# A gated delta-rule layer with a gated MLP on one core: U of the first group in two buffers of its own, weight loads sent behind its copy, fewer dummy products

## The chip, the cores and the metric

The kernel runs on one NeuronCore of a Trainium2 chip. The metric is device time in microseconds of one execution, the median of several runs. TensorE is written PE here (its weight loads PEld), VectorE DVE, ScalarE ACT, GpSimd POOL; SP issues the DMAs.

## The reference

```python
def _attn_ref(q, k, v, beta):               # (4, 8, 768, 48), beta (4, 8, 768)
    k_n = k / (np.linalg.norm(k, axis=-1, keepdims=True) + 1e-06)
    for t in range(S):
        y[:, :, t] = np.einsum('bhd,bhde->bhe', q[:, :, t], state)
        v_old = np.einsum('bhde,bhd->bhe', state, kt)
        state = state + bt[:, :, :, None] * np.einsum('bhd,bhe->bhde', kt, vt - v_old)

def _moe_ref(x, w_gate, w_val, w_out):      # x (3072, 384), d_ff 1536
    gate = 1.0 / (1.0 + np.exp(-(x @ w_gate)))
    val = x @ w_val
    return (gate * val @ w_out)
```
The output of the delta rule, all heads side by side, is the input of the MLP.

## The kernel before

The 768 tokens of each of 32 heads are cut into 12 groups of 64 (`g`, with g = 0 the first). Within a group the recurrence is solved in closed form: products of keys with keys (`gram`, L317), their norms (`norms`, L252), an inverse of a triangular matrix on DVE (`solve_halves`, L410, for groups 0 to 2), and then the corrected values U in two half steps (`updates`, L500): step 0 multiplies the inverse with the first half rows (PE, L518, tile `pu`) and copies them (L521) to `su`; step 1 takes their part from the second half (L510, tile `pk`; `less`, L495, on DVE); step 2 does the second half as step 0 did the first. `su` also holds the state, in the other 64 rows. `rows` (L523) multiplies masked key-query products with `su` for the outputs (tile `yy`, L539), `flip` (L565) transposes them (tile `pt`, L574), `advance` (L547) makes the next state.

The MLP of a group runs tile by tile over d_ff: `gate_val` (L608; tile `gv`, L615 in group 0 and L618 later), sigmoid and product (`gated`, L620), `outp` (L636). One tile is two slots of the loop at L868: in an even slot `gate_val`, in an odd one `outp` of two tiles before. While the MLP of one group runs, the recurrence of the next groups is placed between, by the tables `plan`, `late` and `tail` (L662 to L858). Each table entry names a slot. All orders are written by hand (`manual_schedule`, L699): each engine does its instructions in the order in which the code emits them.

Group 0 has no MLP ahead of it. What PE does there is emitted at L699 to L759, and dummy products (`busy_array`, L102: a bf16 weight load and a product of 512 columns whose result is not used) stand in its idle times. Eight of them are paced: each waits for one instruction of the solve on DVE (`paced`, L448).

The weights come as 36 pieces of 384 KB (`load_piece`, L185), numbered from 0, in the order gate, value, output of each tile. Pieces 0 to 9 are sent at the start. From then on `scaled(n)` (L201, two ACT instructions that unpack piece n) sends piece n + BEHIND, if that is at least EAGER (L209); pieces 10 to 13 are sent behind the copy of U in step 2 (L747). `in_turn` (L111) keeps the number of transfers under way down: from L746 on each waits for the third last one to land. `scaled(n)` of pieces 10 to 35 stand in slots 0 to 18 (L761).

In the trace an f32 product counts as two pairs of weight load and matmul (so the 32 products of a `pu` step are 64 matmuls); a bf16 or f32r one as one pair.

Of the kernel before, what the change touches and what calls it, by code (L numbers as in the profile page):

```python
# [30 lines left out]
J = 8  # L31
# [29 lines left out]
def deltanet_gated_mlp(ctx: ExitStack, tc: tile.TileContext, kd, qd, kv, beta, words, out):  # L61
# [40 lines left out]
    def busy_array(out, n, after=()):  # L102

        for i in range(n):
            ins = nc.tensor.matmul(out=out.rearrange("q a b -> q (a b)"), lhsT=flat[:, 0:128], rhs=flat, start=True, stop=True)  # L105
            if i < len(after):
                pace(ins, after[i])

    sent, behind = [], []

# [299 lines left out]
    def solve_halves(g):  # L410
# [36 lines left out]
        if g == 0:  # L447
            paced = beats[14::2]  # L448
            busy_array(pz, len(paced) + 3, after=paced)
# [13 lines left out]
        if g == 0:  # L463
            gap.append(ps_gv.tile([128, J, C], F32, name="gap", tag="gv"))
            busy_array(gap[0], 3)
        yield
# [4 lines left out]
    def rest(g):  # L471

        st = state[g]
        kq, V = kqp[g % 2], st["kv"][:, 1]
        st["pk"] = pk = [ps_seq.tile([128, J, D], F32, name=f"pk_{g}_{e}", tag="seq") for e in range(2)]
        if g == 0:
            for e in range(2):
                nc.tensor.matmul(out=pk[e].rearrange("q j d -> q (j d)"), lhsT=flat[:, 0:128], rhs=su[:, 2].rearrange("q j d -> q (j d)").bitcast(BF16)[:, 0:J * D],
                                 start=True, stop=True, skip_group_check=True)
        n = 32 if g == 1 else 64  # L480
        for j in range(J if g else 0):
            for a in range(0, 64, n):
                for e, x in KINDS:
                    r, t = 64 * e, tokens_at(e, x) + a
                    m = D // 2 if g == 1 and a == 0 and 0 < j < 4 else D
                    for d in range(0, D, m):
                        nc.tensor.matmul(out=pk[e][t:t + n, j, d:d + m], lhsT=kq[r:r + D, x, j, a:a + n], rhs=su[r:r + D, 2 * x + e, j, d:d + m],  # L487
                                         start=j == 0, stop=True, skip_group_check=True)
        if g == 0:
            st["R"] = [V[:, e * J:(e + 1) * J] for e in range(2)]  # L490
        else:
            st["R"] = [wk.tile([128, J, D], F32, name=f"R_{g}_{e}", tag="row", bufs=3) for e in range(2)]
            less(g)
# [6 lines left out]
    def updates(g, step):  # L500
# [5 lines left out]
        if step == 1:  # L506
            for j in range(J):
                for e, x in KINDS:
                    one, two = to[e, x][0], at[e, x][1]
                    nc.tensor.matmul(out=st["pk"][e][two:two + 32, j], lhsT=L[one:one + 32, x * J + j], rhs=su[one:one + 32, 2 * x + e, j],  # L510
                                     start=False, stop=True, skip_group_check=True)
            less(g)
            return
        pu = [ps_aux.tile([128, J, D], F32, name=f"pu_{g}_{step}_{x}", tag="aux") for x in range(2)]
        for j in range(J):
            for e, x in KINDS:
                i, r = at[e, x][step // 2], to[e, x][step // 2]
                nc.tensor.matmul(out=pu[x][r:r + 32, j], lhsT=mt[i:i + 32, e * J + j], rhs=R[e][i:i + 32, j], start=True, stop=True)  # L518
        for e, x in KINDS:
            r = to[e, x][step // 2]  # L520
            st["u"] = (nc.vector.tensor_copy if g == 0 and x else nc.scalar.copy)(out=su[r:r + 32, 2 * x + e], in_=pu[x][r:r + 32])  # L521

    def rows(g):  # L523
# [7 lines left out]
        n = 32  # L531
        for e in range(2):
            for x in range(2):
                for pair in zip(order[::2], order[1::2]):
                    for a in range(0, 64, n):
                        for j in pair:
                            b, h = head_of(e, x, j)
                            lo = 64 * (b % 2) + a
                            nc.tensor.matmul(out=py[e][lo:lo + n, b // 2, h // 2], lhsT=kq[:, 2 + 2 * e + x, j, a:a + n], rhs=su[:, 2 * x + e, j], start=True, stop=True)  # L539
        st["ys"] = ys = wk.tile([128, 2, H // 2, 2, D], F32, name=f"ys_{g}", tag="ys", bufs=1)  # L540
# [6 lines left out]
    def advance(g):  # L547
# [4 lines left out]
        if 1:  # L552
            pd = [ps_seq.tile([128, J, D], F32, name=f"pd_{g}_{t}", tag="seq") for t in range(2)]
            for j in range(J):
                for e, x in KINDS:
                    r, t = 64 - tokens_at(e, x), below(e)
                    nc.tensor.matmul(out=pd[e][r:r + D, j], lhsT=Kt[t:t + 64, x * J + j], rhs=su[t:t + 64, 2 * x + e, j], start=True, stop=True)  # L557
            for e, x in KINDS:
# [135 lines left out]
    joins, splits = joining(), splitting()  # L694
    EAGER, BEHIND = 14, 8

# [16 lines left out]
    gap.append(ps_gv.tile([128, J, C], F32, name="early", tag="gv"))  # L713
    busy_array(gap.pop(), 5)
    norms0, norms1 = norms(0), norms(1)
# [19 lines left out]
    updates(0, 0)  # L735
    busy_array(gap[0], 5)
    lower_left(1)
# [10 lines left out]
    load_k(2)  # L748
    busy_array(gap[0], 5)
    scaled(9)  # L750
# [18 lines left out]
    spread(splits, 3, 24, 29, into=tail)  # L769
    spread(splits, len(pieces) + 1 - 15, 29, 44, into=tail)  # L770
    tail[18].append(behind.clear)
    for part in (1, 0):
# [144 lines left out]
```

## Time and profile before

| what | before |
|---|---|
| median of 3 runs | 628.56 us (628.52 to 628.64) |
| the profiled execution | 628.08 us |
| its span, first to last instruction | 626.4 us |
| mean granted TensorE clock | 0.996 |
| weight loads sent (36), median from issue to landing | 4.4 us |

A row of the chain of waits gives a start, a length, and the engine, tile and line that held the end; "issue" in it is time in which PE waited for nothing that the profile shows. A row of a timeline gives start, length, engine, line, operation, output and input with their shapes, the count, and in brackets the idle time before it with what ended it. Matmul ends are modelled.

### The profile page before, as it was taken

The numbers are of one execution on the slowest core, as the hardware profiler recorded it, in microseconds if no ns is written. First come the engines' busy times: TensorE is split into PE (matmuls) and PEld (weight loads), VectorE is DVE, ScalarE is ACT, GpSimd is POOL, SyncE is SP. The second block draws the span as 40 slices with busy tenths as digits, with TensorE's granted clock in tenths as the row PEclk, the third lists the DMA queues.
The fourth block names the chain that finished last, engine by engine and source line by source line (L and its number), as shares of the span: only waits on it lengthen the run. The fifth ranks groups of instructions, "written<-read, shape, count | busy, mean of one in ns | idle before, by whom it ended". The sixth has DMA issues, their size and how long they took to land.

```text
span 626.4 us, 25310 instructions
## 1 busy us (share of the span) xinstructions
PE 609.4 (97%) x11126; PEld 565.4 (90%) x11126; DVE 474.4 (76%) x1423; ACT 340.1 (54%) x907; POOL 43.9 (7%) x105
## 2 busy tenths in 40 slices
PE   5889999999999999999999999999999999999996
PEld 4467778899999999999999999999999999999996
DVE  5878786698869879878978978977977977953221
ACT  6759866466446446446446446456456456435322
POOL 6100000000002002002002002002002002001000
PEclk9899999999999999999999999999999999999999
DMA  9478832102112113113113113113113100100101
GB/s 274 170 228 265 281 93 76 31 4 87 28 31 85 27 29 87 26 29 87 27 29 87 27 29 87 27 29 87 27 28 88 27 3 3 26 4 3 26 1 25
DMA packets 17774, 41.14 MB, mean 66 GB/s; under 512 B 4224, under 2 KB 7296, under 8 KB 17664
## 3 DMA queue, kind: packets, MB, share of 16 engines
q1 hardware_dynamic: 17664, 39.53, 21.9%
q8 instruction: 87, 1.43, 1.0%
q14 instruction: 23, 0.19, 0.1%
HBM read 34.80 MB, written 4.72 MB: 63 GB/s over the span
## 4 chain that ended last, share of the span: by engine, by line
PE 90%; DVE 4%; ACT 3%; POOL 1%; issue 1%; ACTq 0%; POOLq 0%
PE gv L618 44%; PE po L649 21%; PE gv L615 5%; PE pu L518 3%; PE yy L539 3%; PE po L643 3%; PE pg L328 2%; PE pp L356 2%; PE pk L487 2%; PE pk L510 1%; PE pd L557 1%; DVE w L236 1%; PE gap L105 1%; PE pm L446 1%; ACT kv L309 1%
## 5 line engine op out<-in xcount | busy, mean ns | idle before, releaser
L618 PE MATMUL gv<-xx,w 128*128 128x256 f32 x2376 | 311.6, 285 | 0.3 <-DVE xx L580 0.3
L618 PEld LDWEIGHTS gv<-xx,w 128*128 128x128 f32 x2376 | 298.9, 191 | 4.0 <-DVE xx L580 0.6
L649 PE MATMUL po<-w,h 128*128 128x384 f32 x792 | 162.7, 341 | 0.0
L649 PEld LDWEIGHTS po<-w,h 128*128 128x128 f32 x792 | 133.8, 188 | 1.2
L629 ACT CAST h<-sg 128x256 fp32r<-128x256 f32 x132 | 53.5, 405 | 116.5 <-DVE sg L624 116.1
L623 ACT ACTIVATE sg<-gv 128x256 f32<-128x256 f32 x144 | 54.9, 381 | 113.1 <-PE gv L618 103.2
L624 DVE TENSOR_TENSOR sg<-sg,gv 128x256 f32<-128x256 f32 x144 | 60.1, 417 | 65.3 <-ACT sg L623 65.0
L384 DVE TENSOR_TENSOR tmp<-X,gp 128x126 f32<-128x126 f32 (+22 forms) x279 | 73.3, 263 | 8.2
L387 DVE TENSOR_TENSOR X<-X,tmp 128x126 f32<-128x126 f32 (+22 forms) x279 | 72.4, 259 | 8.4
L634 DVE TENSOR_TENSOR h<-sg,h 128x256 fp32r<-128x256 f32 x132 | 54.9, 416 | 12.5 <-ACT h L629 12.4
L594 POOL COPY x<-yt 32x192 f32<-32x192 f32 x72 | 29.8, 413 | 443.9 <-DVE yt L589 441.3
L521 ACT COPY su<-pu 32x384 f32<-32x384 f32 x92 | 43.3, 470 | 10.8 <-PE pu L518 9.0
L309 ACT ACTIVATE kv<-kv,mq 128x48 f32<-128x48 f32 x160 | 40.3, 325 | 0.0
L361 DVE TENSOR_TENSOR kqp<-pp,pmask 64x512 f32<-64x512 f32 x48 | 33.0, 689 | 1.4
L615 PE MATMUL gv<-xx,u 128*128 128x256 f32 x144 | 33.7, 385 | 0.1
L615 PEld LDWEIGHTS gv<-xx,u 128*128 128x128 f32 x144 | 26.6, 190 | 4.7 <-ACT xx L577 0.6
L498 DVE TENSOR_TENSOR R<-kv,pk 128x384 f32<-128x384 f32 x44 | 22.4, 550 | 10.0 <-PE pk L510 9.3
L340 ACT COPY G<-pg 32x256 f32<-32x256 f32 (+1 forms) x69 | 25.3, 367 | 7.8 <-PE pg L328 6.4
L594 ACT COPY x<-yt 32x192 f32<-32x192 f32 x72 | 25.1, 349 | 1.2
L589 DVE STREAM_TRANSPOSE yt<-ys 128x768 f32<-128x768 f32 x9 | 8.8, 979 | 20.0 <-ACT ys L545 20.0
L229 ACT CAST w<-u 128x384 fp32r<-128x384 f32 x36 | 18.0, 508 | 9.3 <-DVE w L236 9.2
L563 DVE TENSOR_TENSOR su<-su,pd 48x384 f32<-48x384 f32 x40 | 22.0, 550 | 0.5
(117 smaller groups left out, 544.2 us busy)
## 6 DMA issues: line engine op xcount, KB each, us to landing
raw<-in_words_dram SPq DMA_DIRECT2D x36, 384.0 KB, 4.4
kv<-in_kv_dram SPq DMA_DIRECT2D x24, 384.0 KB, 3.9
kqp<-in_qd_dram SPq DMA_DIRECT2D x24, 256.0 KB, 4.2
kqp<-in_kd_dram SPq DMA_DIRECT2D x24, 192.0 KB, 3.3
out_dram<-ot SPq DMA_DIRECT2D x48, 96.0 KB, 2.2
beta<-in_beta_dram SPq DMA_DIRECT2D x12, 16.0 KB, 3.7
```

The source lines that it names most:

```text
L309: nc.scalar.activation(V[:, c], V[:, c], AF.Copy, scale=mq[:, c, 0:1])
L384: nc.vector.tensor_tensor(out=tmp, in0=X[:, k:16, j:j + 1].to_broadcast([128, n, j]), in1=gp[:, j:j + 1, 0:j].to_broadcast([128, n, j]), o ...
L387: nc.vector.tensor_tensor(out=X[:, k:16, 0:j], in0=X[:, k:16, 0:j], in1=tmp, op=ALU.add)
L521: st["u"] = (nc.vector.tensor_copy if g == 0 and x else nc.scalar.copy)(out=su[r:r + 32, 2 * x + e], in_=pu[x][r:r + 32])
L594: copy(x[32 * q:32 * q + 32, :, :, a].rearrange("q k c s -> q c k s"), yt[32 * a:32 * a + 32, :, q::4])
L615: nc.tensor.matmul(out=pg[:, o], lhsT=parts[w, f][:, k * 128:(k + 1) * 128], rhs=x[0][:, k], start=k == 0, stop=k == KC - 1)
L618: nc.tensor.matmul(out=pg[:, o], lhsT=parts[w, f][:, a, k * 128:(k + 1) * 128], rhs=x[b][:, k], start=(k == 0 and q == 0), stop=(k == KC - ...
L623: nc.scalar.activation(h, st["gv", f][:, 0], AF.Sigmoid)
L624: nc.vector.tensor_tensor(out=h, in0=h, in1=st["gv", f][:, 1], op=ALU.mult)
L629: nc.scalar.copy(hh[:, 0], st["sg", f])
L634: nc.vector.tensor_tensor(out=hh[:, 1], in0=st["sg", f], in1=hh[:, 0].bitcast(F32), op=ALU.subtract)
L649: nc.tensor.matmul(out=po[s], lhsT=hh[:, a, ts], rhs=parts["o", f][:, w], start=(f == 0 and q == 0), stop=(f == NF - 1 and q == 2))
```

## The change

`updates` of group 0 copies all 128 rows of each `pu` bank at once, one bank by ACT and one by DVE, to two tiles `first[0]` and `first[1]` of their own; before, each engine copied two blocks of 32 rows to `su`. Both half steps share the same two `pu` banks, which a dummy product of 384 columns fills beforehand. `rows` and `advance` of group 0 read these tiles (`u_of`), `rows` over 64 rows instead of 128. Dummy products go: three early, five paced, two behind each of the two U steps; of the three gap products two become those that fill the banks. In `rest(1)` six more products are split into halves of 24 columns. EAGER is 17, so that pieces 14 to 16 are no longer sent by `scaled(6)` to `scaled(8)`, but behind pieces 10 to 13 and the keys of group 2. From slot 8 to slot 11 a transfer waits for the second last one instead of the third last.

```diff
@@ busy_array
-            ins = nc.tensor.matmul(out=out.rearrange("q a b -> q (a b)"), lhsT=flat[:, 0:128], rhs=flat, start=True, stop=True)
+            o = out.rearrange("q a b -> q (a b)")
+            ins = nc.tensor.matmul(out=o, lhsT=flat[:, 0:128], rhs=flat[:, 0:o.shape[1]], start=True, stop=True)
@@ solve_halves
-            paced = beats[14::2]
+            paced = beats[24::2]
             busy_array(pz, len(paced) + 3, after=paced)
...
-            busy_array(gap[0], 3)
+            busy_array(gap[0], 1)
+            first_banks()
@@ rest
-                    m = D // 2 if g == 1 and a == 0 and 0 < j < 4 else D
+                    m = D // 2 if g == 1 and a == 0 and (0 < j < 5 or j == 5 and e == 0) else D
@@ updates, step 1
-                    ... rhs=su[one:one + 32, 2 * x + e, j],
+                    ... rhs=u_of(g, e, x)[one:one + 32, j],
@@ updates, steps 0 and 2
-        pu = [ps_aux.tile([128, J, D], F32, name=f"pu_{g}_{step}_{x}", tag="aux") for x in range(2)]
+        pu = st["pu"] if g == 0 else [ps_aux.tile([128, J, D], F32, name=f"pu_{g}_{step}_{x}", tag="aux") for x in range(2)]
...
+        if g == 0:
+            for x, copy in enumerate((nc.scalar.copy, nc.vector.tensor_copy)):
+                st["u"] = copy(out=first[x], in_=pu[x])
+            return
         for e, x in KINDS:
             r = to[e, x][step // 2]
-            st["u"] = (nc.vector.tensor_copy if g == 0 and x else nc.scalar.copy)(out=su[r:r + 32, 2 * x + e], in_=pu[x][r:r + 32])
+            nc.scalar.copy(out=su[r:r + 32, 2 * x + e], in_=pu[x][r:r + 32])
+
+    def first_banks():
+
+        state[0]["pu"] = [ps_aux.tile([128, J, D], F32, name=f"pu_0_{x}", tag="aux") for x in range(2)]
+        for bank in state[0]["pu"]:
+            busy_array(bank, 1)
+        first.extend(wk.tile([128, J, D], F32, name=f"u_0_{x}", tag="row", bufs=3) for x in range(2))
+
+    def u_of(g, e, x):
+        return su[:, 2 * x + e] if g else first[x]
@@ rows
+            k = slice(0, 128) if g else slice(below(e), below(e) + 64)
-                            ... lhsT=kq[:, 2 + 2 * e + x, j, a:a + n], rhs=su[:, 2 * x + e, j], start=True, stop=True)
+                            ... lhsT=kq[k, 2 + 2 * e + x, j, a:a + n], rhs=u_of(g, e, x)[k, j], start=True, stop=True)
@@ the order of the start
-    EAGER, BEHIND = 14, 8
+    EAGER, BEHIND = 17, 8
-    busy_array(gap.pop(), 5)
+    busy_array(gap.pop(), 2)
...
     updates(0, 0)
-    busy_array(gap[0], 5)
+    busy_array(gap[0], 3)
...
     stage(10, 14, state[0]["u"])
     load_k(2)
-    busy_array(gap[0], 5)
+    stage(14, 17)
+    busy_array(gap[0], 3)
...
+    for s, n in ((8, 2), (11, 3)):
+        plan[s].append(lambda n=n: behind.__setitem__(0, n))
```

On ACT, from the first U copy to the outputs of group 0 (`raw` are the weight pieces that `scaled` unpacks, two instructions each), the order before was

```order
L521 COPY su<-pu_0_0_526 32x384 [waits PE_49]
L521 COPY su<-pu_0_0_526 32x384
L400 ACTIVATE scratch<-G_281,under 128x16x16
L206 ACTIVATE raw_120<-raw_120 128x384 [waits DMAHW2_49]
L208 ACTIVATE raw_120<-raw_120 128x384
L206 ACTIVATE raw_122<-raw_122 128x384 [waits DMAHW3_49]
L208 ACTIVATE raw_122<-raw_122 128x384
L521 COPY su<-pu_2_0_623 32x384 [waits PE_49]
L521 COPY su<-pu_2_0_623 32x384
L206 ACTIVATE raw_124<-raw_124 128x384 [waits DMAHW4_49]
```
and now, at the same place of ACT:

```order
L523 COPY u_0_511<-pu_0_507 128x384 [waits PE_49]
L401 ACTIVATE scratch<-G_278,under 128x16x16
L207 ACTIVATE raw_120<-raw_120 128x384 [waits DMAHW2_49]
L209 ACTIVATE raw_120<-raw_120 128x384
L207 ACTIVATE raw_122<-raw_122 128x384 [waits DMAHW3_49]
L209 ACTIVATE raw_122<-raw_122 128x384
L523 COPY u_0_511<-pu_0_507 128x384 [waits PE_49,Activation_49]
L207 ACTIVATE raw_124<-raw_124 128x384 [waits DMAHW4_49]
```
The two copies of each step have become one of 128 rows, and nothing else has moved; DVE changes in the same way.

On PE, from the last product of U's second step to the outputs, the order before had five dummy pairs (`gap<-dmask`) ahead of these rows, and the outputs `yy` read `su`:

```order
L539 MATMUL yy_0_687<-su,kqp_76 32x48 [waits PE_49,Activation_49]
L539 MATMUL yy_0_687<-su,kqp_76 32x48 x15
L539 MATMUL yy_0_687<-su,kqp_76 32x48 [waits DVE_49]
L539 MATMUL yy_0_687<-su,kqp_76 32x48 x15
L539 MATMUL yy_1_688<-su,kqp_76 32x48 [waits DVE_49,PE_49]
L539 MATMUL yy_1_688<-su,kqp_76 32x48 x31
```
Now three dummy pairs stand ahead of them:

```order
L556 MATMUL yy_0_671<-u_0_511,kqp_76 32x48 [waits Activation_49]
L556 MATMUL yy_0_671<-u_0_511,kqp_76 32x48 x15
L556 MATMUL yy_0_671<-u_1_512,kqp_76 32x48 [waits DVE_49]
L556 MATMUL yy_0_671<-u_1_512,kqp_76 32x48 x15
L556 MATMUL yy_1_672<-u_0_511,kqp_76 32x48 [waits PE_49]
L556 MATMUL yy_1_672<-u_0_511,kqp_76 32x48 x15
L556 MATMUL yy_1_672<-u_1_512,kqp_76 32x48 x16
```
The 64 products are the same in number; each half now reads the tile that one engine copied, and waits for that engine alone.

On SP, behind the ten pieces of the start (`raw_124` is piece 9), the loads before stood so (`kqp_76` from `in_kd_dram` are the keys of group 2; DMAHW are landings of earlier transfers):

```order
L188 DMA raw_446<-in_words_dram 128x768 [waits DMAHW5_49,Activation_49]
L188 DMA raw_572<-in_words_dram 128x768 [waits DMAHW6_49,Activation_49]
L188 DMA raw_576<-in_words_dram 128x768 [waits DMAHW7_49,Activation_49]
L188 DMA raw_661<-in_words_dram 128x768 [waits DMAHW5_49,DMAHW0_49,DVE_49]
L188 DMA raw_663<-in_words_dram 128x768 [waits DMAHW6_49,DMAHW1_49]
L188 DMA raw_665<-in_words_dram 128x768 [waits DMAHW7_49,DMAHW2_49]
L188 DMA raw_667<-in_words_dram 128x768 [waits DMAHW3_49,DMAHW0_49]
L119 DMA kqp_76<-in_kd_dram 48x1024 [waits DMAHW4_49,DMAHW1_49,PE_49]
L119 DMA kqp_76<-in_kd_dram 48x1024 [waits DMAHW2_49,PE_49]
L188 DMA raw_678<-in_words_dram 128x768 [waits DMAHW3_49,Activation_49]
```
and now

```order
L189 DMA raw_641<-in_words_dram 128x768 [waits DMAHW5_49,DMAHW2_49,DVE_49]
L189 DMA raw_643<-in_words_dram 128x768 [waits DMAHW6_49,DMAHW3_49]
L189 DMA raw_645<-in_words_dram 128x768 [waits DMAHW7_49,DMAHW4_49]
L189 DMA raw_647<-in_words_dram 128x768 [waits DMAHW5_49,DMAHW0_49]
L120 DMA kqp_76<-in_kd_dram 48x1024 [waits DMAHW6_49,DMAHW1_49,PE_49]
L120 DMA kqp_76<-in_kd_dram 48x1024 [waits DMAHW7_49,PE_49]
L189 DMA raw_651<-in_words_dram 128x768 [waits DMAHW0_49]
L189 DMA raw_653<-in_words_dram 128x768 [waits DMAHW1_49]
L189 DMA raw_655<-in_words_dram 128x768 [waits DMAHW2_49]
L189 DMA raw_662<-in_words_dram 128x768 [waits DMAHW3_49,Activation_49]
```
The three pieces that waited for ACT alone (14 to 16: `raw_446`, `raw_572`, `raw_576`) have moved behind the four that wait for the copy of U on DVE and behind the keys; the last row of both is piece 17.

More of the change, by code (lines that the diff above doesn't have):

```diff
@@ L104, in busy_array @@
         for i in range(n):
-            ins = nc.tensor.matmul(out=out.rearrange("q a b -> q (a b)"), lhsT=flat[:, 0:128], rhs=flat, start=True, stop=True)
+            o = out.rearrange("q a b -> q (a b)")
+            ins = nc.tensor.matmul(out=o, lhsT=flat[:, 0:128], rhs=flat[:, 0:o.shape[1]], start=True, stop=True)
             if i < len(after):
                 pace(ins, after[i])
-    sent, behind = [], []
+    sent, behind, first = [], [], []
     def in_turn(ins):
@@ L509, in updates @@
                     one, two = to[e, x][0], at[e, x][1]
-                    nc.tensor.matmul(out=st["pk"][e][two:two + 32, j], lhsT=L[one:one + 32, x * J + j], rhs=su[one:one + 32, 2 * x + e, j],
+                    nc.tensor.matmul(out=st["pk"][e][two:two + 32, j], lhsT=L[one:one + 32, x * J + j], rhs=u_of(g, e, x)[one:one + 32, j],
                                      start=False, stop=True, skip_group_check=True)
@@ L517, in updates @@
                 i, r = at[e, x][step // 2], to[e, x][step // 2]
-                nc.tensor.matmul(out=pu[x][r:r + 32, j], lhsT=mt[i:i + 32, e * J + j], rhs=R[e][i:i + 32, j], start=True, stop=True)
+                nc.tensor.matmul(out=pu[x][r:r + 32, j], lhsT=mt[i:i + 32, e * J + j], rhs=R[e][i:i + 32, j], start=True, stop=True, skip_group_check=g == 0)
+        if g == 0:
+            for x, copy in enumerate((nc.scalar.copy, nc.vector.tensor_copy)):
+                st["u"] = copy(out=first[x], in_=pu[x])
+            return
         for e, x in KINDS:
             r = to[e, x][step // 2]
-            st["u"] = (nc.vector.tensor_copy if g == 0 and x else nc.scalar.copy)(out=su[r:r + 32, 2 * x + e], in_=pu[x][r:r + 32])
+            nc.scalar.copy(out=su[r:r + 32, 2 * x + e], in_=pu[x][r:r + 32])
[6 more added lines that the diff above has]
+        return su[:, 2 * x + e] if g else first[x]
     def rows(g):
@@ L538, in rows @@
                             lo = 64 * (b % 2) + a
-                            nc.tensor.matmul(out=py[e][lo:lo + n, b // 2, h // 2], lhsT=kq[:, 2 + 2 * e + x, j, a:a + n], rhs=su[:, 2 * x + e, j], start=True, stop=True)
+                            nc.tensor.matmul(out=py[e][lo:lo + n, b // 2, h // 2], lhsT=kq[k, 2 + 2 * e + x, j, a:a + n], rhs=u_of(g, e, x)[k, j], start=True, stop=True)
         st["ys"] = ys = wk.tile([128, 2, H // 2, 2, D], F32, name=f"ys_{g}", tag="ys", bufs=1)
@@ L556, in advance @@
                     r, t = 64 - tokens_at(e, x), below(e)
-                    nc.tensor.matmul(out=pd[e][r:r + D, j], lhsT=Kt[t:t + 64, x * J + j], rhs=su[t:t + 64, 2 * x + e, j], start=True, stop=True)
+                    nc.tensor.matmul(out=pd[e][r:r + D, j], lhsT=Kt[t:t + 64, x * J + j], rhs=u_of(g, e, x)[t:t + 64, j], start=True, stop=True)
             for e, x in KINDS:
```

## The prediction

> **What bounds the kernel now.** I read the page first, then the chain of waits in order of time over the first 90 us, then the windows and the timeline of each engine where that chain breaks. All times are microseconds from the start of the span.
>
> ```profile
> PE 609.4 (97%) x11126; PEld 565.4 (90%) x11126; DVE 474.4 (76%) x1423; ACT 340.1 (54%) x907; POOL 43.9 (7%) x105
> ```
> ```profile
> q8 instruction: 87, 1.43, 1.0%
> ```
> ```profile
> 70.00:626.00 556.00, 550.16 (x9677) 1.00 0.16 44
> ```
> The third fence is a row of the windows view of PE: window, length, busy time, count, granted clock, DMA share, GB/s. From 70 on PE is busy 550.16 of 556: what starts earlier there ends earlier. The change touches only what lies ahead, and there the chain shows this:
>
> ```profile
> 27.70 0.97 PE gap L105 x4
> 28.67 0.32 issue
> 28.99 0.38 PE gap L105
> 29.37 0.81 PE pk L510 x64
> ...
> 32.18 0.54 issue
> 32.72 0.28 PE pu L518 x5
> 33.00 1.18 PE gap L105 x5
> 34.18 1.41 PE yy L539 x117
> 35.59 1.27 issue
> 36.87 0.36 PE yy L539 x11
> ...
> 37.98 0.83 PE pt L574 x6
> ...
> 39.56 5.42 PE gv L615 x24
> ...
> 65.51 0.58 issue
> ```
> Columns: start, length, what. Four times PE stops with "issue", in the middle of a group whose data is there (117 of 128 yy products, then a stop, then 11). The spacing tells what it is:
>
> ```profile
> 25.29:28.99 3.70, 3.29 (x127) 1.00 0.37 103
> 28.99:32.72 3.73, 3.18 (x129) 1.00 0.38 118
> 32.72:36.87 4.15, 2.88 (x128) 1.00 0.64 194
> ```
> Between stops lie 127 to 129 matmuls, each with its weight load: 256 instructions. The page's instruction queue moved 87 packets for 2 x 11126 PE instructions: also 256 a packet (1.43 MB / 87 = 16.4 KB). So PE waits for its **code**. A portion took 3.70 us where PE stood waiting for each, 4.15 where loads ran beside it.
>
> When code is sent for can be seen in the DMA view (queue: packets, MB, share), here of 26.38 to 26.40, then of 41.70 to 41.75 (of 36.87 to 41.70 it lists no packet of that queue):
>
> ```profile
> q8 instruction: 1, 0.02, 437.8%
> ```
> ```profile
> q8 instruction: 1, 0.02, 120.2%
> ```
> After the stop that ended at 25.29 the next packet started at 26.39, 1.1 later, and PE had it at 28.99, 2.6 after that. After the resume at 36.87, with three weight loads under way, it started only at 41.7: 4.8 later.
>
> [...]
>
> **The change part by part.** *U in its own buffers.* The copies now, of ACT and then of DVE:
>
> ```profile
> 32.95 0.95 ACT L521 COPY su<-pu 32x384 f32<-32x384 f32 x2 [1.81 <-PE pu L518]
> ...
> 36.26 0.46 ACT L545 COPY ys<-yy 128x384 f32<-128x384 f32 x1
> ```
> ```profile
> 30.29 1.02 DVE L498 TENSOR_TENSOR kv<-kv,pk 128x384 f32<-128x384 f32 x2 [0.64 <-issue]
> ...
> 33.04 1.14 DVE L521 COPY su<-pu 32x384 f32<-32x384 f32 x2 [1.13 <-PE pu L518]
> ...
> 37.26 0.56 DVE L543 COPY ys<-yy 128x384 f32<-128x384 f32 x1 [1.60 <-PE yy L539]
> ```
> A 128-row copy of 384 columns takes 0.46 (ACT) and 0.56 (DVE), no more than one of 32 rows (0.48, 0.57). One instead of two takes 0.48 and 0.58 off each step, on the path twice.
>
> *Fewer dummy products.* Ahead of yy 12 go (3, 5, 2, 2; one gap product becomes two into the U banks, 3 as before). Each is a weight load and a matmul, so every boundary of 256 instructions lands 24 instructions, or 12 small matmuls, later in the work. Of yy 11 matmuls stood behind the last boundary; now all 128 stand ahead of it and the boundary falls at the end of the three dummies behind them. The earlier one moves from pu's 59th matmul over three dummies to yy's third, the one before from the dummies to pk's tenth. Waits for code now fall where PE waits for a copy anyway.
>
> *The sum.* The boundary in pm comes 8 matmuls later (five plus three dummies gone), so 25.4 for 25.29. For the next two portions I take 3.5 each, an estimate between the 3.73 of the second row and the 3.18 that PE was busy in it (in less time code would not be waited for), since no load is sent any more between the first ten pieces and the second U copy; these two are its ends. For the third 4.0, between 3.70 and 4.15, as the loads start with it; its ends are 3.18 and 7.2 (4.8 + 2.4, the slow packet above).
> 1. pu ends at 27.7 as before (dummies follow at 27.70). U is there at 27.8 + 0.56 = 28.4, pk starts at 28.5, does 10 of 64 matmuls, waits for code until 25.4 + 3.5 = 28.9, and ends at 28.9 + 54/64 x 0.81 = 29.6 (was 30.18).
> 2. R takes DVE 1.02 with hand-overs of 0.1: 30.75. The second pu runs without the 0.54 and ends at 31.6 (was 33.00).
> 3. Three dummies (3/5 of 1.18) end at 32.3, the DVE copy of U (0.56) at 32.2. yy starts at 32.35, waits for code until 28.9 + 3.5 = 32.4, and ends at 33.95 (was 37.23).
> 4. ACT ended its U copy at 33.90 and started ys at 36.26, with a weight piece and a table load between, 2.36. From 32.1 that is 34.5, and ys ends at 34.95. pt could start at 35.1, but the code behind the boundary comes at 32.4 + 4.0 = 36.4. So pt starts at **36.4 instead of 37.98**, and gv 1.58 later as before: -1.6.
>
> *yy on 64 rows* is not in the trace; its pace of 12 ns a matmul (1.41 / 117) is that of pk (0.81 / 64), so I put it at 0, within 0.1 either way, hidden by the wait for code.
>
> *Pieces 11 to 17 behind the copy.* They are 10 to 16 in the code's count from 0; four were sent behind the copy already, three ahead of it.
>
> ```profile
> 34.21 1.77 SPq L188 DMA_DIRECT2D raw<-in_words_dram  x2
> ```
> All seven now start from 32.3, with the two K loads of group 2 ahead of the last three. I put it at 0: the four that ACT and DVE meet first were sent from 34.21 and are now sent 1.9 earlier for a need that is 1.6 earlier. But three more loads stand ahead of every later one: 384 KB at the 194 GB/s of the third row is 2.0 each, 6.0 in all, less 1.9: up to 4.1 later. Cover: in the chain ACT and DVE are nowhere held by one of them. If it is gone, ACT stops at the first late piece, and behind it on ACT stands the sigmoid that frees PE's next gv bank; the other bank holds one tile of work, 2.7 (half of 5.42), so PE loses at most 4.1 - 2.7 = 1.4.
>
> *Two at a time.* On SP, pieces 29 to 34 and one kv load wait for the one before last instead of the third last. It may shorten the wait for code at 65.51: from 0.3 worse to its whole 0.58; I take -0.15.
>
> *Six products of pk(1) split in two.* Twelve matmuls more on the path:
>
> ```profile
> 55.17 1.63 PE L487 MATMUL pk<-su,kqp 48*32 48x48 f32 x152
> ```
> 12 x 10.7 ns = +0.13 (0 to 0.13). They put the boundaries behind them back where they were.
>
> ```profile
> span 626.4 us, 25310 instructions
> ```
> Together -1.6 - 0.15 + 0.13 = -1.6. The profiled execution took 628.08, 1.68 more than its span, so 626.5; the median of the runs is 628.56, 0.48 above it, so **627.0**. About 0.2% (1.26 us) is what a measurement here can tell from no change; faster means below 627.3.
>
> **The rivals.** *Code that arrives early* (the fetch gets ahead of the first new load, a portion of 3.2 us): pt waits for ys alone, at 35.1 to 35.4; gain up to 2.9 with a better wait at 65.51. 625.5 to 626.3; taken as 626.0.
>
> *The array stays at half clock.* The windows view of all engines, clock in the third last column:
>
> ```profile
> 16.00:18.00 2.00, 1.13 (x3) 0.30 (x3) 1.74 (x8) 1.91 (x6) 0.00 (x0) 0.80 1.05 407
> 18.00:20.00 2.00, 2.00 (x5) 0.41 (x4) 1.71 (x9) 1.91 (x6) 0.00 (x0) 0.50 1.04 415
> 20.00:22.00 2.00, 1.72 (x16) 0.69 (x16) 1.79 (x6) 1.54 (x4) 0.37 (x1) 0.85 0.49 198
> ```
> ```profile
> 19.27 0.10 PEld L105 LDWEIGHTS <-dmask 128*128 128x128 bf16 x1 [0.38 <-DVE tmp L429]
> ```
> 0.80, 0.50 and 0.85 are 0.8, 2.0 and 0.6 us at half clock: down at 17.2, up at 20.6, 3.4 us apart, after idle time and then eight paced dummies. Now the first paced one is that of 19.27, so 1.3 us of work stand ahead of 20.6. If that does not lift the clock, the next chance is 24.0. Price: up to 0.4 on the dummies and, if the rate halves, 1.2 on pz (64 matmuls in 2.05 now). Of 0.3 to 1.6 the waits for code swallow some 0.3, so about 0.8: 627.7.
>
> [...]
>
> *Code behind the loads.* If two pieces pass ahead of the third packet, pt starts near 37.2: 628.0. *Late loads*, with half of the 1.4 above, give 627.6 to 627.7.
>
> *The slower side.* The third packet is held back as at 36.87, 4.8 us, since the first loads are sent in the same microsecond as the request. Then code comes at 32.4 + 4.8 + 2.4 = 39.6 and pt starts 1.6 later than before: 630.1. It decides from a start of the packet later than 35.6, 3.2 after the boundary. Against it: at 32.72 as well a load was under way, and that portion took 4.15.
>
> *The change does nothing:* only if the boundaries do not move by 24 instructions; the counts of 127 to 129 speak against it.
>
> **How the numbers follow.** Forecast 0.42 (626.4 to 627.5, a seventh of it above 627.3); early code 0.17; half clock 0.16 (a fifth below 627.3); code behind two pieces 0.12; late loads 0.05; slower 0.08. Faster: 0.36 + 0.17 + 0.03 = 0.56. Same: 0.06 + 0.13 + 0.12 + 0.05 = 0.36. Slower: 0.08. The range 625.8 to 628.4 leaves out the slower case, a third of early code and a little of the clock case, under 2 in 10.
>
> **What would show it.** Right: "issue" stops in pk and near the start of yy, none in pu, yy in one piece, a last stop behind yy that ends near 36.4; U copies of 128 rows once per engine and step; gv from 38.0; PE from there as before. Wrong: a clock of 0.50 after 20.6; an "issue" stop behind yy of over 3 us; ACT or pg waiting for loads between 42 and 70; a wait at 65.51 grown beyond 0.9.

## The result and the profile after

| what | before | after |
|---|---|---|
| median, on the same chip | 628.54 us (6 runs, 626.51 to 628.71) | 631.3 us (6 runs, 630.43 to 632.89) |
| ratio, 95% interval | | 1.0055 [1.0035, 1.0075] |
| the profiled execution | 628.08 us | 632.89 us |
| its span | 626.4 us | 631.2 us |

The changed kernel is slower by 0.55%, some 2.8 us in the median. Its profiled execution was the slowest of the six, so differences read from its rows are larger than those of the medians.

The chain of waits of the changed kernel, as before in order of time (start, length, what):

```profile
19.94 2.32 PE pz L106 x5
22.26 3.56 PE pz L456 x64
...
29.70 0.88 PE pu L520 x63
...
31.33 0.24 PE pk L512 x9
31.57 0.10 issue
...
35.26 0.20 PE yy L556 x2
35.46 0.21 issue
35.68 1.52 PE yy L556 x120
...
37.73 3.32 issue
41.05 0.58 PE gap L106
41.63 1.28 PE pt L591 x6
42.91 1.28 PE gap L106 x3
44.19 5.83 PE gv L632 x24
```
The stops for code ("issue") stand where the prediction put them: in pk behind the ninth product, in yy behind the second, and behind yy (one dummy ahead of the place named); yy is no longer cut near its end. But pz takes 3.56 (before 2.05), pu starts at 29.70 (26.82), and the stop behind yy is 3.32 long. So pt starts at 41.63 instead of 37.98, 3.65 later, where 36.4 was forecast. gv comes at 44.19 instead of 39.56, 4.6 later: pt and the dummies behind it take 2.56 instead of 1.58.

The windows view of the same kernel (window, length, then busy time of PE, PEld, DVE, ACT, POOL, then granted clock, DMA share, GB/s):

```profile
22.00:26.00 4.00, 4.00 (x66) 3.62 (x66) 3.68 (x5) 0.14 (x1) 1.78 (x2) 1.00 0.03 9
38.00:42.00 4.00, 0.95 (x4) 0.75 (x4) 0.72 (x2) 0.00 (x0) 0.00 (x0) 0.57 0.80 277
42.00:50.00 8.00, 8.00 (x39) 6.13 (x40) 5.16 (x19) 3.89 (x10) 0.00 (x0) 0.79 0.82 266
80.00:631.00 551.00, 544.90 (x9593) 519.84 (x9592) 416.81 (x1247) 283.92 (x780) 30.39 (x73) 1.00 0.16 43
```
From 80 on PE is busy 544.90 of 551, the same share as before: the loss lies ahead. From 38.6, 0.8 into the long stop, to 45.4 the array is at half clock again: 0.57 and 0.79 are 3.4 us of half clock in each row, 6.8 in all. The first row has to be read with care. It says 1.00, but the five dummies ahead of pz took 2.32, some 0.46 each (0.43 at half clock, where three took 1.28; 0.22 at full clock, where three took 0.65 in the kernel before), and pz takes 3.56: the array is at half clock. The first clock record in this trace is the rise at 28.3, and ahead of it the column is not to be believed.

The copies of U became what was said, one of 0.48 on ACT and one of 0.56 on DVE, from the two timelines:

```profile
34.59 0.48 ACT L523 COPY u<-pu 128x384 f32<-128x384 f32 x1 [1.20 <-PE pu L520]
```
```profile
34.59 0.56 DVE L523 COPY u<-pu 128x384 f32<-128x384 f32 x1 [0.40 <-PE pu L520]
```
The DMA view shows why the last stop is long. Of 35.69 to 38.67 it lists weight loads, and no packet of PE's code; of 38.67 to 38.75 it has the packet:

```profile
q8 instruction: 1, 0.02, 74.9%
```
So from PE's crossing into the next portion at 35.68 to the start of the packet it took 3.0, and PE had it 2.4 later. After the boundary at 25.29 in the kernel before, with no loads under way, the lag was 1.1.

### The profile page after: what moved, and what is told of

It reads as the page before. It is cut to its first block, busy times and chain, and to the rows that moved or that the text cites. A ratio compares the mean times of both kernels' runs of the same rounds, so it can differ in the third digit from the quotient of the medians.

```text
span 631.2 us, 25294 instructions
## 1 busy us (share of the span) xinstructions
PE 608.4 (96%) x11119; PEld 568.0 (90%) x11126; DVE 473.9 (75%) x1421; ACT 339.3 (54%) x905; POOL 44.1 (7%) x105
## 4 chain that ended last, share of the span: by engine, by line
PE 90%; DVE 6%; issue 1%; ACT 1%; DMA 1%; ACTq 0%; SPq 0%; DVEq 0%
PE gv L635 44%; PE po L666 21%; PE gv L632 5%; PE pu L520 3%; PE yy L556 3%; PE po L660 3%; PE pg L329 2%; PE pp L357 2%; PE pk L489 2%; PE pk L512 1%; PE pd L574 1%; DVE w L237 1%; PE gap L106 1%; PE pm L447 1%; DMA kqp<-in_kd_dram 1%
## 5 line engine op out<-in xcount | busy, mean ns | idle before, releaser
L527 ACT COPY su<-pu 32x384 f32<-32x384 f32 x88 | 41.5, 471 | 8.2 <-PE pu L520 6.4
```

The costliest lines, as they stand in the source:

```text
L527: nc.scalar.copy(out=su[r:r + 32, 2 * x + e], in_=pu[x][r:r + 32])
```

## The experiments

Ratios are to the kernel before on the same chip (its median there was 627.68 to 628.15), with 95% intervals. Positions are from one profiled execution each.

**The changed kernel with its first five paced dummies back.** The same number fewer elsewhere keeps the portions' boundaries behind them:

```diff
-            paced = beats[24::2]
-            busy_array(pz, len(paced) + 3, after=paced)
+            paced = beats[14::2]
+            busy_array(pz, len(paced), after=paced)
...
-    gap.append(ps_gv.tile([128, J, C], F32, name="early", tag="gv"))
-    busy_array(gap.pop(), 2)
```


> The changed kernel with eight paced dummy products again (from the seventh step of the solve on), and five others (two early, three behind the paced ones) left out instead, so that every boundary of 256 PE instructions falls on the same product as in the changed kernel. Theory 1 (the array stays at half clock until 28.3 because the paced products start too late): pz takes about 2.0 us instead of 3.56, the first U products start near 26.8 instead of 29.7, and the time falls by 2 to 3 us to 628.4 to 629.3, with the stop behind yy (3.3 us) still there. Rival (the slow clock is hidden, since code sets the pace anyway): pz is fast, but the transposes stay near 41.6 and the time near 631.

630.62, ratio 1.0043 [1.0026, 1.0059]. From PE's timeline (the bracket is the idle time before the group) and from the chain:

```profile
16.58 4.05 PE L106 MATMUL pz<-dmask 128*128 128x512 bf16 x8 [4.44 <-DVE tmp L430]
21.55 2.73 PE L456 MATMUL pz<-mt,wide 64*64 64x32 f32 x47 [0.92 <-ACT raw L209]
```
```profile
21.55 3.63 PE pz L456 x64
...
36.94 3.04 issue
```
The second row is cut at the end of its window, with 47 of 64 products. Work from 16.58 on did not lift the clock: pz is as slow as in the changed kernel, and neither the time nor the start that the theory expected came. What is missing against the kernel before are the three unpaced dummies, and PE idles 0.92 just ahead of pz; that this is the reason is argued here, not shown.

**The changed kernel with its loads late.** Pieces 10 to 17 are sent behind the next pair of ACT instructions (`scaled(9)`):

```diff
-    EAGER, BEHIND = 17, 8
+    EAGER, BEHIND = 18, 8
...
-    stage(10, 14, state[0]["u"])
-    load_k(2)
-    stage(14, 17)
     busy_array(gap[0], 3)
     scaled(9)
+    stage(10, 14, done[9])
+    load_k(2)
+    stage(14, 18)
```


> The changed kernel with pieces 10 to 17 sent behind the unpacking of piece 9 on ACT instead of behind the U copy, about 0.9 us later. Theory 2 (the code behind yy is held back because three loads are sent just ahead of its request): the code packet gets ahead of the loads, the stop behind yy shrinks from 3.3 to about 1.0 to 1.6 us, the array does not fall back to half clock there, and the time falls by 2 to 4 us to 627.3 to 629.3. Rival (a portion of code takes this long whatever the loads do): the stop stays at 3 us, the time near 631 or above.

629.17, ratio 1.0026 [1.0003, 1.0049]. The chain:

```profile
22.06 2.61 PE pz L456 x64
...
35.06 1.30 issue
...
36.73 0.66 PE pt L591 x6
...
40.69 3.75 DMA kqp<-in_kd_dram
```
The stop behind yy is 1.30 instead of 3.32, and pt starts at 36.73. But pz, on which the edit has no bearing, is faster as well, so this execution had luck with the clock; and PE now waits 0.6 for the keys of group 2, which come late. The windows of this kernel show that luck:

```profile
20.00:22.00 2.00, 2.00 (x7) 0.45 (x6) 1.79 (x6) 1.51 (x4) 0.37 (x1) 0.50 0.43 170
22.00:24.00 2.00, 2.00 (x49) 2.00 (x48) 1.97 (x3) 0.00 (x0) 1.58 (x2) 0.65 0.04 11
```
The same dummies as in the changed kernel, and the clock rose near 23.4; there it rose at 28.3.

**Both edits.**

```diff
+            paced = beats[14::2]
+            busy_array(pz, len(paced), after=paced)
...
+    stage(10, 14, done[9])
+    load_k(2)
+    stage(14, 18)
```


> Both edits. If the two causes add: pz fast, a stop behind yy of 2 us or less, the transposes at 35.5 to 36.8 instead of 41.6, time 625.5 to 627.3, faster than the kernel before. If one of them hides the other: no better than the better of the two alone.

630.51, ratio 1.0038 [1.0020, 1.0055], where 625.5 to 627.3 was expected if both causes went. The chain:

```profile
21.54 3.63 PE pz L456 x64
...
37.26 1.67 issue
...
39.51 1.28 PE pt L591 x6
```
The stop is halved, and the kernel is still slow: the stop behind yy alone does not make the loss. The other cause was not removed, as pz is still cold.

**U alone.** The kernel before with the copies to `first[0]` and `first[1]`; dummies, loads and splits as before:

```diff
+        if g == 0:
+            for x, copy in enumerate((nc.scalar.copy, nc.vector.tensor_copy)):
+                st["u"] = copy(out=first[x], in_=pu[x])
+            return
```


> The kernel before with U in its own two buffers and nothing else (all dummies, loads and splits as before), so the boundaries of 256 instructions stay where they were (dummies, 59th matmul of the second U step, 118th of yy). If code sets the pace there (boundaries at 25.3, 29.0, 32.7, 36.9): the copies are 0.5 us shorter, the stops in pu and yy grow by as much, time 628.2 to 628.6. Rival (the copies are on the path): the transposes start 0.7 to 1.2 us earlier, time 627.3 to 627.9.

628.45, ratio 1.0001 [0.9987, 1.0015]. No gain. The chain still has the stops of the kernel before:

```profile
29.23 0.37 issue
...
32.79 0.54 issue
...
36.17 1.16 issue
```
Two copies less on each step move no boundary, so PE meets the same stops.

**The cut alone.** The kernel before with the dummies of the changed kernel and the six splits, U and loads as before:

```diff
-            paced = beats[14::2]
+            paced = beats[24::2]
...
-    busy_array(gap.pop(), 5)
+    busy_array(gap.pop(), 2)
...
-                    m = D // 2 if g == 1 and a == 0 and 0 < j < 4 else D
+                    m = D // 2 if g == 1 and a == 0 and (0 < j < 5 or j == 5 and e == 0) else D
```


> The kernel before with only the dummy products cut and six products of pk split, as in the change (U, loads and their order as before). If the cut is the cause, by the slow clock and by moving the code boundary to where the loads start: the array comes to full clock later than in the kernel before, a stop of over 2 us behind yy, time 629.5 to 632. Rival (the cut matters only together with the seven loads behind the copy): 627.5 to 628.7.

629.63 (before 627.68), ratio 1.0030 [1.0016, 1.0045]. The chain:

```profile
21.88 3.56 PE pz L455 x64
...
38.23 1.79 issue
```
The cut costs some 1.9 us by itself, with the cold pz of 3.56; the stop behind yy is 1.79, where over 2 was expected.

**Loads alone.** The kernel before with pieces 14 to 16 behind the K loads:

```diff
-    EAGER, BEHIND = 14, 8
+    EAGER, BEHIND = 17, 8
...
     load_k(2)
+    stage(14, 17)
```


> The kernel before with only pieces 14 to 16 moved behind pieces 10 to 13 and the keys of group 2. The request for code at the 59th matmul of the second U step goes out before the U copy ends, so it stands ahead of the loads: the stop in yy is 1.3 or less, and with no load before it the stops of 0.3 and 0.5 shrink by up to 0.3 each; time 627.3 to 628.4. Rival (the loads themselves cost: ACT or the key products wait for them): over 629.

628.31, ratio 1.0007 [0.9996, 1.0019]: no difference. pt started at 37.09, 0.9 earlier, as the stop in yy shrank from 1.27 to 0.73 and the one ahead of pk from 0.32 to 0.05; it was given back behind (a stop of 0.58 at 89.30 that the kernel before does not have).

**All but the cut.** The changed kernel with all dummies and splits of the kernel before:

```diff
-            paced = beats[24::2]
+            paced = beats[14::2]
...
-    busy_array(gap.pop(), 2)
+    busy_array(gap.pop(), 5)
...
-    updates(0, 0)
-    busy_array(gap[0], 3)
+    updates(0, 0)
+    busy_array(gap[0], 5)
```


> The changed kernel with all dummies and splits of the kernel before: U in its own buffers, loads behind the copy, two at a time. If the cut alone is the cause, the loss is gone: 626.8 to 628.5. If the loads cost by themselves: 629.5 or more.

628.94, ratio 1.0024 [1.0007, 1.0042]. pz took 2.30 and pt started at 37.51, 0.47 earlier than in the kernel before. Yet the time lies between the two cases expected, and is no better: the chain now leads through weight loads (4.30 and 2.80 at 64.93 and 69.30) to ACT and from there to PE.

**Two at a time alone**, in the kernel before:

```diff
+    for s, n in ((8, 2), (11, 3)):
+        plan[s].append(lambda n=n: behind.__setitem__(0, n))
```


> The kernel before with only two transfers at a time in slots 8 to 11. The stop near 65.5 (0.58) shrinks or goes: 627.4 to 628.2. Rival (no effect, as the six loads start only when that code is already there): within 0.3 of the kernel before.

628.12, ratio 1.0009 [0.9999, 1.0018]. The stop near 65.7 shrank from 0.58 to 0.07, and one of 0.55 came up at 89.32.

**The changed kernel, kept warm.** The eleven dummies that run up to pz as before, eight paced and three not, and five fewer elsewhere (one of them among the early ones), so that the boundaries stay:

```diff
-            paced = beats[24::2]
+            paced = beats[14::2]
             busy_array(pz, len(paced) + 3, after=paced)
...
-            busy_array(gap[0], 1)
             first_banks()
...
-    busy_array(gap.pop(), 2)
+    busy_array(gap.pop(), 1)
...
     updates(0, 0)
-    busy_array(gap[0], 3)
```


> The changed kernel with the stand-in matmuls ahead of the first group's pz as they were before (paced from the 14th stamp on, so three unpaced ones right ahead of pz again), and as many taken out behind: one of the two early ones, the one at the gap bank ahead of the banks, the three behind the updates. The instruction boundaries behind pm fall where they fall in the changed kernel; the loads too are as in the changed kernel. Theory (the cut ahead of pz lets the array fall to half clock, and the loads hold the code packet behind yy; two causes): pz starts near 21.7 and takes near 2.1 instead of 3.56, U's copies 2 to 3 earlier than in the changed kernel, but the stop behind yy stays at 3 or a little more; 628.5 to 629.5, that is 1.5 to 2.5 below the changed kernel. [...] Rival (the stop behind yy only came because pz was late): the stop falls to 1 or less, 627.

629.97, ratio 1.0027 [1.0006, 1.0048]; 626.24 to 633.47. The chain of its profiled execution, which took 626.98:

```profile
21.98 1.99 PE pz L456 x64
...
34.55 1.85 issue
```
pz is back to what it was. The stop behind yy was 1.85 in this execution, not 3. The runs spread over 7 us and this is one of the shortest, so its rows say little of the median.

**Kept warm, and the loads late:** the edits of the run before and of the run with late loads.

```diff
+            paced = beats[14::2]
...
+    stage(10, 14, done[9])
+    load_k(2)
+    stage(14, 18)
```


> The run before with the pieces 10 to 17 sent behind the second scaled half, as in the run with late loads. Theory of two causes: pz near 2.1, the stop behind yy 1.3 or less, pt at 34.5 to 36 where the kernel before has it at 37.98, and K's loads waited for near 40 as in the run with late loads (0.6 or less); 626.5 to 627.7, level with the kernel before or up to 1.5 faster. Rival (a third cause, the late loads for ACT at 61 to 76 that the run with all stand-ins showed): 628.5 to 629.5 although PE is ahead of the kernel before at pt. Rival (cold clock again): 629 or more with pz near 3.5.

628.73, ratio 1.0022 [1.0000, 1.0044]. pt started at 37.30, 0.7 ahead of the kernel before; PE waited 0.3 at pp (near 74.6) for copies of ACT that had waited for weight loads. That is the third cause of the expectation. Its size can't be read here: the profiled execution (627.56) was the fastest of 12, the median 1.2 above it.

**The same with three transfers at a time:**

```diff
-    for s, n in ((8, 2), (11, 3)):
-        plan[s].append(lambda n=n: behind.__setitem__(0, n))
```


> The run before without the two transfers at a time in slots 8 to 11 (three, as in the kernel before). Theory: if two at a time holds the raw loads back for ACT at 61 to 76, this gains 0.5 to 1 on the run before, 626 to 627; if it does nothing, the two are within 0.3.

628.08 (before 628.15), ratio 1.0001 [0.9988, 1.0014]: the loss is gone. The chain:

```profile
32.47 1.66 PE yy L555 x121
...
34.66 1.95 issue
...
36.99 0.66 PE pt L590 x6
```
Here the plan of the prediction can be seen at work: pt at 36.99, and PE did not wait for loads. This execution took 626.98, the fastest of 11.

**All but the cut, with three at a time:** the run with all dummies, without

```diff
-    for s, n in ((8, 2), (11, 3)):
-        plan[s].append(lambda n=n: behind.__setitem__(0, n))
```


> The run with all stand-ins and splits of the kernel before, own buffers for U and early loads, now without the two transfers at a time. That run took 0.24 per cent more than the kernel before, while each of its three parts alone took no more. Theory (two transfers at a time on top of a stage that begins early leaves the loads late for ACT, DMA raw on the chain at 65 to 72): without it 627.5 to 628.3, level with the kernel before, and the chain has no DMA at 61 to 72. Rival (early loads and U together slow something else, such as the code packets): it stays 0.2 per cent above the kernel before.

628.92, ratio 1.0013 [1.0001, 1.0025]. The theory that two at a time makes the loads late fell: they are late with three as well. ACT's timeline of this run:

```profile
70.26 0.55 ACT L207 ACTIVATE raw<-raw 128x384 int32<-128x384 uint16 x1 [1.77 <-DMA raw<-in_words_dram]
...
73.75 1.93 ACT L527 COPY su<-pu 32x384 f32<-32x384 f32 x4
```
and of the kernel before:

```profile
73.10 1.93 ACT L521 COPY su<-pu 32x384 f32<-32x384 f32 x4 [0.40 <-PE pu L518]
```
Before, ACT waited 0.40 there for PE. Now ACT waits 1.77 for a load, its copies come 0.65 later than before, and PE waits for them. So the next limit stood 0.40 behind PE all the time: with these loads, what PE gains in the first 70 us beyond 0.4 is taken back here. It need not be: in the run before this one PE was 1.5 ahead and did not wait.

**The changed kernel with three at a time**, that same edit alone.

```diff
-    for s, n in ((8, 2), (11, 3)):
-        plan[s].append(lambda n=n: behind.__setitem__(0, n))
```


> The changed kernel without the two transfers at a time in slots 8 to 11 (three, as in the kernel before). Theory (the cold clock at pz and the held packet are the loss of this kernel, and PE is too late at 60 to 80 for a late load to matter): within 0.6 of the changed kernel, 630.5 to 631.5. Rival (two at a time costs on its own): 629 to 630, 1.3 to 2 below the changed kernel, as the pair with and without it behind the restored stand-ins gave 0.7 to 1.3.

630.1, ratio 1.0031 [1.0016, 1.0047]. The chain:

```profile
22.05 2.28 PE pz L456 x64
...
35.07 2.49 issue
...
38.15 1.28 PE pt L591 x6
...
40.71 6.45 PE gv L632 x24
```
That is nearer to the rival's 629 to 630: two at a time seems to cost by itself. The rows show something else too. pz was nearly warm by luck, and in the stop of 2.49 the array fell back to half clock: pt took 1.28 instead of 0.66, gv 6.45 instead of 5.42. From 36.3 to 43.1, with the fall 1.2 into the stop, is an estimate in steps of 3.4 us from the rise at 22.7 (granted 0.84 from 22 to 24).

**Kept warm, loads early, three at a time:**

```diff
+            paced = beats[14::2]
...
-    for s, n in ((8, 2), (11, 3)):
-        plan[s].append(lambda n=n: behind.__setitem__(0, n))
```


> The changed kernel with the stand-ins ahead of pz as before (as many fewer behind) and three transfers at a time, the loads early as in the changed kernel. The same with two at a time took 629.97, ratio 1.0027. If two at a time is what is left of the loss: 628 to 628.6, ratio 1.000 to 1.001. If the early loads are (they hold the code packet behind yy in some executions): 629.5 or more, ratio 1.002 or more.

629.12, ratio 1.0018 [1.0003, 1.0033], between the two cases. PE waited 0.39 and 0.65 at pp for ACT: late loads with three at a time, as above. The array also fell back to half clock with no long stop ahead of it, as four dummies show that took 0.46 each; from 29.8 to 33.2 is an estimate from these rows and from the pu behind them, 1.30 instead of 0.88:

```profile
29.05 0.39 issue
...
30.52 1.82 PE gap L106 x4
```
This version and the one above with its loads late differ in the order of the loads alone: 1.0018 against 1.0001.

**Half the instructions in yy.** The kernel before with one product for 64 rows of queries instead of two for 32:

```diff
-        n = 32
+        n = 64 if g == 0 else 32
```


> The kernel before with the first group's yy in products of 64 rows of queries instead of 32: 64 instead of 128 products with the same result, 128 instructions less with their weight loads. Theory (code sets the pace at 28 to 37): the boundary that stops the kernel before inside yy (1.27) and one portion of 3.7 halves go, so pt starts 1.2 to 1.9 earlier than 37.98, and if the loads and ACT follow, 626.3 to 627.3; if they bind at pp (near 75), the gain shrinks to 0.3 to 0.8. Rival (PE waits for U or for other data, the stops are a side effect): pt within 0.3 of 37.98 and the time within 0.6 of the kernel before.

637.94, ratio 1.0166 [1.0139, 1.0192]: 10 us slower. The chain:

```profile
34.30 2.00 PE yy L539 x64
...
37.06 0.84 PE pt L574 x6
...
45.80 3.10 issue
...
49.66 4.47 PE gv L615 x12
...
70.48 2.13 issue
...
74.51 4.12 PE gv L615 x12
```
The stop in yy is gone and pt starts 0.92 earlier (1.2 was the least expected; a product of 64 rows took 31 ns, one of 32 rows 12). But all boundaries behind have moved by half a portion: stops of 3.10 in pd and 2.13 in pm come up, and behind them a gv takes 4.47 (2.79 before) or 4.12 (2.59) in stretches that are partly at half clock (granted 0.67 from 48.9 to 54, 0.77 from 72.6 to 80). The two stops are 5.2 and the two slow gv 3.2 more; two more stops of 1.1 follow at 122.8 and 126.4, while 1.85 of stops of the kernel before are gone. The rest of the 10 was not traced.

**The same on the version kept warm, loads late, three at a time:**

```diff
-        n = 32
+        n = 64 if g == 0 else 32
```


> The changed kernel with the stand-ins ahead of pz restored, the loads late and three transfers at a time (it took 628.08, ratio 1.0001, pt at 36.99), and the first group's yy in 64 products instead of 128. Theory (code): no stop ahead of pt, pt near 34.5 to 35.2, and 626 to 627, level with or faster than the run before it in this call; if K's loads or the loads for ACT bind, a wait at pg (near 40) or pp (near 73) of 0.5 to 2 takes most of it back and the time stays at 627.3 to 628. Rival (the stop of 1.95 moves with the boundary and is paid elsewhere): a stop of 1 or more between pg and pd and 628.

635.99, ratio 1.0126 [1.0113, 1.0139]. pt started at 36.26, where the theory had 34.5 to 35.2; a stop of 3.44 in pd and one of 1.28 in pm follow: the rival, that the stop moves with the boundary, and dearer than it put it. No version beat the kernel before.

## Why the prediction was wrong

*Code bounds PE, and the boundaries move by 12 products: right.* The stops came at the places named. U alone moves none of them and gains nothing. With the array kept warm, the loads late and three at a time, PE resumed behind yy at 36.61 (34.66 + 1.95) where the prediction had 36.4, and pt started at 36.99, one dummy behind. That the first number fits so well is partly luck: the loads were sent later there than in the kernel that the sum describes.

*The cold array was the step that failed.* The prediction had "1.3 us of work stand ahead of 20.6", took that to lift the clock, and so let pu end at 27.7 as before, with 0.16 for the other case and "about 0.8" as its price. Both were wrong. 20.6 was the moment of one execution: the same instructions gave a pz of 3.56 (changed kernel), 2.61 (loads late) and 2.28 (three at a time), with the clock rising at 28.3, 23.4 and 22.7. The 24.0 of the next chance was an estimate, 20.6 + 3.4.

With all eleven dummies ahead, pz took 1.99 to 2.06 in eight profiled executions and 2.30 to 2.47 in four; with six, 2.28 to 3.56 in four; with eight and the gap, 3.63 in both. So the eleven make pz nearly independent of that moment, and the cut took this away. An account of how, by the author's estimate: in the traces of the two kernels the changes of clock lie multiples of 3.4 us apart (17.2 and 20.6 before; 28.3, 38.6 and 45.4 after). Reckoned back from the rise in such steps, an interval began at 20.0 and 19.3 with late loads and with three at a time, near the first dummy (19.27), and the clock rose at its end; in the changed kernel and with the cut alone (a rise near 30.5, estimated from its slow rows) an interval ended at 21.5 and 20.3, among the dummies, and neither the interval ahead of it nor the one behind it, filled with the rest of the dummies and then pz, brought the rise.

The price, which the prediction put on a few dummies and pz, ran through every group up to pu, 2.9 in the profiled execution; "the waits for code swallow some 0.3" of it, it had said. By medians there are six comparisons with and without the cut, where all else is equal up to other dummies and the six splits: alone 0.30%; on all the rest 0.31% (1.0055 against 1.0024) and, with three at a time, 0.18% (1.0031 against 1.0013); against the versions kept warm 0.28% (1.0055, 1.0027), 0.13% (1.0031, 1.0018) and 0.04% (1.0026, 1.0022). All have one sign; the mean is 0.21%, 1.3 us, of the 2.8 that the median lost. The first is the direct one and clear of noise; the others are differences of two ratios, and share runs.

*The packet behind loads* was seen, at 0.08, as a rival of its own. Its start, 3.0 behind the boundary, is a little under the 3.2 from which it was to decide, and the portion took 5.37 (35.68 to 41.05), within the bounds of 3.18 to 7.2 but above the 4.0 taken. By itself it would have put pt near 38, level with before. The rivals were priced one by one, as if they excluded each other; they came together: of the 5.2 that pt was later than forecast, 3.3 is the boundary crossed late (35.68 instead of 32.4, the cold array and what follows from it), 1.4 the portion, and 0.6 a cold dummy between resume and pt. And the array fell back to half clock at the stop, which no rival counted: 6.8 us in the changed kernel. How much of the median the loads alone take is not settled: sending them late lowered the ratio by 0.29, 0.05, 0.05 and 0.17 points in the four pairs, of which none is sure by itself; the mean is 0.14%, 0.9 us.

*Two at a time,* taken at -0.15, has the wrong sign. Five pairs differ in it alone: 0.24 (changed kernel), 0.09 (kept warm), 0.21 (kept warm, loads late), 0.11 (all dummies) and 0.09 points (kernel before), all for three at a time. No pair is sure by itself, but all have one sign; the mean is 0.15%, 0.9 us. Where it is lost was not found: the stop near 65.5 did shrink, as forecast, and the late loads at pp come with three at a time as well.

*Late loads,* at 0.05 and with a cover of 2.7 of work, were underrated for the case that PE is early. The cover that counts is the 0.40 by which ACT waited for PE at its copies near 73. In the changed kernel itself PE is 4 us late there, and the loads do not bind.

*The sizes that were right:* copies of 0.48 and 0.56, the six splits (pk of group 1 takes 0.11 longer, 1.67 instead of 1.56, for +0.13), and the boundary near 65.5, whose stop is gone.

The ladder of medians: 1.0055 for the change, 1.0027 with the eleven dummies ahead of pz restored, 1.0022 with the loads late, 1.0001 with three transfers at a time. The three together are the loss, as its ends, 1.0055 [1.0035, 1.0075] and 1.0001 [0.9988, 1.0014], show. How it divides among them is less sure: with three at a time first, the loads take 0.17 points (1.0018 to 1.0001) instead of the 0.05 of this ladder.

## What to carry to other kernels

Work that only keeps the array busy, right ahead of many small products, is not idle filling (without five of eleven such dummies pz took 3.56 instead of 2.05 here): before taking it out, ask what happens if the clock rises later than in the one trace at hand (at 20.6 before, at 28.3 after). Where PE waited for its code, a shorter wait for data gained nothing (U alone, 1.0001), and instructions taken out moved the later stops (half the instructions in yy, new stops of 3.10 and 2.13): look up where each will fall, beside which loads, and how busy PE is ahead of it. Rivals that share a cause, or follow one another on the path, have to be priced together as well.

## What the runs showed of the hardware

The moments at which the clock changes lie multiples of 3.4 us apart in the traces of the two kernels (17.2 and 20.6 in the kernel before; 28.3, 38.6 and 45.4 in the changed kernel), and fall differently in each execution: with the same instructions ahead, the clock rose at 28.3 (changed kernel), 23.4 (loads late) and 22.7 (three at a time), and the time of pz was 3.56, 2.61 and 2.28; runs of one version spread by up to 8 us (627.56 to 635.54, kept warm and the loads late). Of two busy stretches of 3.4 us, reckoned back from the rise, one lifted the clock and one did not: in the changed kernel PE was busy all through from 21.49 to 24.91, first with 0.8 of dummies and then with small products of pz, and the clock rose only at 28.3; with late loads 2.1 of dummies and 1.3 of pz, from 19.98 to 23.39, ended with the rise. That the share of dummies decides is not shown.

Half clock followed stops for code of 2.13 and 3.10 (half the instructions in yy, clock 0.77 and 0.67 behind them), 2.49 (three at a time, pt 1.28), 3.04 (paced dummies back, pt 1.28), 3.32 (changed kernel, clock 0.50 from 38.6) and 3.44 (kept warm with half the yy, gv 5.17). It came 0.8 into that of 3.32, by estimate 1.2 into that of 2.49, and in two executions at a place where no stop was over 0.4 (kept warm, loads early, three at a time, near 29.8; kept warm with half the yy, near 30.6, where pu took 1.50 instead of 0.88; both moments estimated from the slow rows). In the 3.4 us that ended in these four falls PE was busy 2.2, 2.2, 2.1 and 2.5, in large part with small products; the first is from the windows view, the others are added up from the rows of the chains. A stop of 1.67 was followed by half clock once (both edits, where pt took 1.28) and once not (kept warm, loads late, pt 0.66); those of 1.79 (the cut alone, pt 0.66), 1.85 (kept warm, pt 0.66) and 1.95 (kept warm, loads late, three at a time, pt 0.66) were not.

A packet of code started 1.1 us after PE crossed a boundary where no loads ran (kernel before, at 25.29), and 3.0 (changed kernel, at 35.68) and 4.8 us (kernel before, at 36.87) after it behind fresh weight loads.
